# A transformer block, forward and backward: dq kept in SBUF for half of the tokens, the dqkv transposes moved ahead of the last stage, dx interleaved with the last dWqkv pass

## The chip, the cores and the metric

The kernel runs on one core of a Trainium2 chip. The metric is device time in microseconds, the median of several runs. A core has TensorE (PE: matmuls, and PEld: weight loads), VectorE (DVE), ScalarE (ACT), GpSimd (POOL) and SyncE (SP); matmuls write to PSUM, all else lives in SBUF or in DRAM. In this kernel three engines issue DMAs: SP (`LD`), ACT (`AQ`) and POOL (`ST`).

## The reference

One pre-LN block with its gradients, in bf16: sequence S = 2048, width D = 512, 32 heads of 16, MLP width F = 1792. Attention of a token looks at W = 8 tokens, two apart: `idx = pos[:, None] - 2 * arange(8)[None, :]`, masked below zero.

```python
h = x + _A_ref(_layernorm(x), A_wqkv, A_wo)
h2 = h + _B_ref(_layernorm(h), B_w1, B_b1, B_w2, B_b2)   # gelu MLP
```

The kernel returns h2 and the gradients dx, dWqkv, dWo, dW1, db1, dW2, db2. At the end of the backward pass, with ln1 the normalized x: dq = sum over the window of ds times k; dWqkv = ln1^T [dq dk dv]; dln1 = [dq dk dv] Wqkv^T; and dx is the LayerNorm backward of dln1, plus dh.

## The kernel before, in words

A token tile is 128 tokens on 128 partitions, so there are NT = 16 of them, and NPR = 8 pairs. D makes DT = 4 tiles of 128, 3D makes JT = 12. The program runs through stages: LN1 and a weight permutation, QKV and attention with LN2 (phases B and C), the MLP forward and backward (D), dW2, dWo and dO, then four stages that matter here.

**H (L706 to L795)** goes through the pairs and forms ds, which stays in SBUF (`ds_tiles`), and dk and dv, by matmuls with shift matrices into PSUM (`sacc`), an ACT cast (`res_sb`, L722) and a POOL store to DRAM (`dk_d`, `dv_d`).

**dW1** is spread over H and E2 by two helpers. `d3b_load` (L592) loads a 128x512 piece of dh1 on ACT's queue (`dh1c`, L600) and transposes it on TensorE (`tpd`). `d3b_mm` (L604) does one of 16 output blocks: 16 matmuls (L617), an ACT cast (`dw_sb`, L620) and a POOL store (L621). Their buffers are in the pools of the stack `d3`, on the right side of SBUF, closed at L833.

**E2 (L802 to L832)** forms dq. For each pair it loads KL (L812, eight loads of 256 KB on SP, one for each window position, two buffers); for each of the two tiles VectorE multiplies by ds (`pk`, L817), adds eight terms to four (L821), to two (L823), to one (`dq_sb`, L825), and POOL stores the tile to `dq_d` (L826). Two blocks of dW1 follow each pair. After pair 2, 16 loads on ACT's queue (L831) bring ln1 back as `xh1_tm`.

**K (L839 to L910)** comes when E2's and d3's pools are closed. It loads the weights `wqp` (L848) and dk (L851) on SP, dv on ACT (L853), and dq half on POOL, half on SP (L855), as column blocks of `dqkv_tm[st]`, one [128, 1536] tile for each token tile. Twelve groups of four TensorE transposes make WqkvT. Then the loop over `jc in [1, 2, 0]` (dk, dv, dq): for each token tile, four matmuls into the four banks of one PSUM tile `dwqkv_ps` (L865) and one group of four transposes of the same block into `dqkvT`, and after 16 tiles four casts, on ACT (L872) and VectorE (L874) by turns, and four POOL stores (L875). At last 16 dx tiles: twelve matmuls into `dln_ps` (L880), an ACT pass that sums rows (L891), six VectorE instructions (L894 to L908) and a POOL store (L910).

A group of transposes goes through `pe_T` (L130): four transposes into one PSUM tile (`tps`, two buffers), then one copy to SBUF by ACT or VectorE (L135).

The order on each engine is the scheduler's, which places instructions by their dependences and priorities; it is not always the program's order. In the profile and the order, `xh` is xh1_tm, `ln_d` is ln1_d and ln2_d, `dqkv` a tile of dqkv_tm, `t` the partial sums of E2.

Of the kernel before, what the change touches and what calls it, by code (L numbers as in the profile page):

```python
# [38 lines left out]
def build(ctx, tc, A_x, A_wqkv, A_wo, B_w1, B_b1, B_w2, B_b2, grad_out,  # L39
# [762 lines left out]
    with tc.tile_pool(name="i_big", bufs=2) as i_big, \  # L802
            tc.tile_pool(name="i_pv", bufs=2) as i_pv, \
            tc.tile_pool(name="i_t", bufs=2) as i_t, \
            tc.tile_pool(name="i_io", bufs=4) as i_io, \
            tc.tile_pool(name="ps_w1b", bufs=2, space=bass.MemoryType.PSUM) as ps_w1b:
        for pr in range(NPR):
            tok0 = pr * PS2
            KL = i_big.tile([P, W, 2, D], BF16, name="KL")
            for w in range(W):  # L810
                r0 = PAD + tok0 - 2 * w
                LD.dma_start(out=KL[:, w, :, :], in_=k_tm_d[r0:r0 + PS2, :].rearrange("(k p) d -> p k d", p=P))  # L812
            for k in range(2):
                t = pr * 2 + k
                ts0 = t * P
                pk = i_pv.tile([P, W, DH, H], BF16, name="pk")
                nc.vector.tensor_tensor(out=pk[:], in0=KL[:, :, k, :].rearrange("p w (d h) -> p w d h", d=DH, h=H),  # L817
                                        in1=ds_tiles[t][:, :, None, :].to_broadcast([P, W, DH, H]), op=ALU.mult)
                pk3 = pk[:].rearrange("p w d h -> p w (d h)")
                t1 = i_t.tile([P, 4, D], BF16, name="t1")  # L820
                nc.vector.tensor_tensor(out=t1[:], in0=pk3[:, 0:4, :], in1=pk3[:, 4:8, :], op=ALU.add)  # L821
                t2 = i_t.tile([P, 2, D], BF16, name="t2")
                nc.vector.tensor_tensor(out=t2[:], in0=t1[:, 0:2, :], in1=t1[:, 2:4, :], op=ALU.add)  # L823
# [3 lines left out]
                dbg_tm('dq', t, r_sb[:], i_io)  # L827
            d3b_mm(2, ps_w1b)
            if pr == 2:
                for st in range(NT):  # L830
                    AQ.dma_start(out=xh1_tm[st][:], in_=ln1_d[st * P:(st + 1) * P, :])  # L831
        d3b_mm(len(d3_work), ps_w1b)  # L832
    d3.close()  # L833
    if dbg.get('stop_after') == 'E':
        fpre_cm.__exit__(None, None, None)
        dsp_cm.__exit__(None, None, None)
        return

    with tc.tile_pool(name="k_w", bufs=1) as k_w, \  # L839
# [9 lines left out]
        dqkv_tm = [k_w.tile([P, 3 * D], BF16, name=f"dqkv_{i}") for i in range(NT)]  # L849
        for st in range(NT):  # L850
            LD.dma_start(out=dqkv_tm[st][:, D:2 * D], in_=dk_d[st * P:(st + 1) * P, :])  # L851
        for st in range(NT):
            AQ.dma_start(out=dqkv_tm[st][:, 2 * D:3 * D], in_=dv_d[st * P:(st + 1) * P, :])  # L853
        for st in range(NT):
            (nc.gpsimd if st % 2 == 0 else LD).dma_start(out=dqkv_tm[st][:, 0:D], in_=dq_d[st * P:(st + 1) * P, :])  # L855
# [4 lines left out]
        dqkvT = k_w.tile([P, JT, S], BF16, name="dqkvT")  # L860
        for jc in [1, 2, 0]:
            dw_ps = ps_kw.tile([P, DT, D], F32, name="dwqkv_ps")
            for st in range(NT):
                for ct in range(DT):
                    nc.tensor.matmul(dw_ps[:, ct, :], lhsT=xh1_tm[st][:, ct * P:(ct + 1) * P],  # L865
                                     rhs=dqkv_tm[st][:, jc * D:(jc + 1) * D], start=(st == 0), stop=(st == NT - 1))
# [2 lines left out]
            for ct in range(DT):
                w_sb = k_io.tile([P, D], BF16, name="dwqkv_sb")  # L870
                if ct % 2 == 0:
                    nc.scalar.copy(out=perm_view(w_sb[:]), in_=dh_view(dw_ps[:, ct, :]))  # L872
                else:
                    nc.vector.tensor_copy(out=perm_view(w_sb[:]), in_=dh_view(dw_ps[:, ct, :]))  # L874
                ST.dma_start(out=out_dwqkv[ct * P:(ct + 1) * P, jc * D:(jc + 1) * D], in_=w_sb[:])  # L875
        for t in range(NT):
# [92 lines left out]
```

## Time and profile before

| | us |
|---|---|
| median of 5 runs | 1091.3 |
| lowest and highest | 1087.05, 1096.33 |
| profiled execution | 1092.42 |
| its span, first to last instruction | 1090.7 |
| granted TensorE clock, mean over the span | 0.890 |

The profile is one execution; times in it count from the start of its span. A row of the timeline has start, length, engine, line, operation, tile written and tiles read, a count, and in brackets the idle time ahead of it and what ended that. ACTq and SPq are the DMA issues of those queues.

### The profile page before, as it was taken

How to read it: one execution, taken by the hardware profiler on the slowest of the kernel's cores; microseconds unless marked ns; L12 is line 12 of the kernel's file. 1: busy time of each engine (PE TensorE's matmuls, PEld its weight loads, DVE VectorE, ACT ScalarE, POOL GpSimd, SP SyncE). 2: the span in 40 equal slices, each digit the busy share in tenths (PEclk: the TensorE clock that was granted, in tenths of full speed). 3: DMA queues.
4: the chain of work that ended last, by engine and by line, in shares of the span. 5: the costliest groups of instructions: out<-in, count | busy, mean ns of one | idle time of the engine just before them, and what ended most of it. 6: DMA issues, size and time to landing. Idle time of an engine off the chain costs nothing. (4 is left out here: it accounts for less than half of the span.)

```text
span 1090.7 us, 14749 instructions
## 1 busy us (share of the span) xinstructions
PE 813.4 (75%) x5145; PEld 401.5 (37%) x5234; DVE 703.1 (64%) x1448; ACT 415.6 (38%) x745; POOL 214.5 (20%) x402
## 2 busy tenths in 40 slices
...
GB/s 256 145 174 155 244 156 196 183 130 83 11 44 98 54 87 68 36 96 40 49 111 63 109 172 46 94 80 81 97 66 59 314 311 246 224 90 20 20 77 68
DMA packets 102893, 126.87 MB, mean 116 GB/s; under 512 B 14977, under 2 KB 90530, under 8 KB 102818
## 3 DMA queue, kind: packets, MB, share of 16 engines
...
q14 instruction: 34, 0.28, 0.1%
...
## 5 line engine op out<-in xcount | busy, mean ns | idle before, releaser
L421 PE MATMUL dl_ps<-w1T,dh 128*128 128x512 bf16 x217 | 63.1, 413 | 17.9 <-DVE t L443 17.3
...
L479 PE MATMUL h_ps<-ln2T_all,w 128*128 128x512 bf16 x220 | 62.1, 387 | 6.4 <-ACT c1u L484 4.7
L518 PE MATMUL dg_ps<-dYTg,w2T 128*128 128x512 bf16 x216 | 62.2, 381 | 5.7 <-DVE db1part L521 4.8
L500 PE MATMUL y_ps<-w,gch 128*128 128x512 bf16 x218 | 58.0, 384 | 5.3 <-DVE gch L496 4.8
L701 PE MATMUL sacc<-pvE,SC 128*128 128x512 bf16 x223 | 57.0, 398 | 0.2 <-issue 0.2
L695 PE MATMUL sacc<-pvE,SD 128*128 128x512 bf16 x203 | 52.3, 393 | 6.3 <-DVE pvE L786 5.4
L135 ACT COPY dh_tmA<-tpd 128x512 bf16<-128x512 bf16 x56 | 32.5, 586 | 64.2 <-PE tpd L134 61.8
L880 PE MATMUL dln_ps<-wqkvT,dqkvT 128*128 128x512 bf16 x187 | 47.3, 400 | 10.9 <-DVE k_t L903 10.3
L617 PE MATMUL dw_ps<-dh_tmA,ln_tm 128*128 128x512 bf16 (+1 forms) x241 | 52.6, 361 | 2.7 <-ACT dw_sb L620 0.8
L134 PE MATMUL tps<-ident,xhat 128*128 128x128 bf16 x128 | 16.3, 275 | 49.1 <-DVE xhat L177 34.2
L865 PE MATMUL dwqkv_ps<-dqkv,xh 128*128 128x512 bf16 x184 | 52.0, 409 | 1.0 <-DMA dqkv<-dk_d 0.5
L323 PE MATMUL acc<-pv,ident 128*128 128x512 bf16 x123 | 40.0, 474 | 15.0 <-DVE pv L319 14.6
L817 DVE TENSOR_TENSOR pk<-KL,ds_t 128x4096 bf16<-128x4096 bf16 x16 | 35.9, 2285 | 23.1 <-DMA KL<-k_tm_d 21.8
L722 ACT CAST res_sb<-sacc 128x512 bf16<-128x512 f32 x32 | 18.7, 585 | 82.7 <-PE sacc L695 76.2
L482 ACT ACTIVATE u<-h_ps,b1col 128x512 bf16<-128x512 f32 x56 | 38.3, 685 | 19.1 <-DMA w<-in_B_w_dram 5.9
L277 DVE TENSOR_TENSOR prod<-kTg,qTg 128x1024 bf16<-128x1024 bf16 x64 | 40.0, 678 | 7.1 <-ACT kTg L236 7.1
L134 PE MATMUL tpd<-ident,dh1c 128*128 128x128 bf16 x224 | 24.1, 234 | 27.3 <-DMA dh1c<-dh_d 18.6
L521 DVE CUSTOM_DVE_ANT_0 dh<-dg_ps,gd 128x512 bf16<-128x512 f32 x56 | 38.3, 684 | 7.3 <-PE dg_ps L518 6.6
L747 DVE TENSOR_TENSOR prodA<-vT,doT 128x1024 bf16<-128x1024 bf16 x64 | 42.3, 681 | 0.5
L421 PEld LDWEIGHTS <-dh 128*128 128x128 bf16 x224 | 23.2, 104 | 47.4 <-issue 26.6
L319 DVE TENSOR_TENSOR pv<-VL,a_bf 128x4096 bf16<-128x4096 bf16 x16 | 36.3, 2278 | 6.5 <-DMA VL<-v_tm_d 3.7
...
## 6 DMA issues: line engine op xcount, KB each, us to landing
VL<-v_tm_d SPq DMA_DIRECT2D x64, 256.0 KB, 5.2
KL<-k_tm_d SPq DMA_DIRECT2D x64, 256.0 KB, 5.4
dh_d<-dh POOLq DMA_DIRECT2D x72, 128.0 KB, 2.1
dh1c<-dh_d ACTq DMA_DIRECT2D x56, 128.0 KB, 2.4
x_sb<-in_A_x_dram SPq DMA_DIRECT2D x32, 128.0 KB, 3.6
ln_d<-xhat POOLq DMA_DIRECT2D x32, 128.0 KB, 2.8
dh_r<-dh_d SPq DMA_DIRECT2D x32, 128.0 KB, 2.2
out_dram<-dw_sb POOLq DMA_DIRECT2D x26, 128.0 KB, 2.4
```

The costliest lines, as they stand in the source:

```text
L134: nc.tensor.transpose(ps[:, i, :], s, ident[:])
L277: nc.vector.tensor_tensor(out=prt[:], in0=win, in1=qT[:, jt:jt + 1, s_off:s_off + PS2].to_broadcast([P, 4, PS2]), op=ALU.mult)
L421: nc.tensor.matmul(dl_ps[:], lhsT=dh1_list[ft][:, tt * P:(tt + 1) * P], rhs=W1T_sb[ft][:], start=(ft == 0), stop=(ft == FT - 1))
L479: nc.tensor.matmul(h1_ps[:], lhsT=W1_sb[ct][:, ft * P:(ft + 1) * P], rhs=ln2T_all[:, ct, sc * GS:(sc + 1) * GS], start=(ct == 0), stop=(ct ...
L500: nc.tensor.matmul(y_ps[:, tt, :], lhsT=gch[:, tt * P:(tt + 1) * P], rhs=W2_sb[ft][:], start=(ft == 0), stop=False)
L518: nc.tensor.matmul(dg_ps[:], lhsT=W2T_sb[dt][:, ft * P:(ft + 1) * P], rhs=dYTg[:, dt, :], start=(dt == 0), stop=(dt == DT - 1))
L617: nc.tensor.matmul(ps[:, 0:fl], lhsT=ln2_tm[st][:, ct * P:(ct + 1) * P], rhs=dh1_tmA[:, st, f0:f0 + fl], start=(st == 0), stop=(st == NT - 1))
L695: nc.tensor.matmul(acc_list[t - 1][:], lhsT=SDm[w][:], rhs=rhs[w], start=False, stop=(w == W - 1))
L701: nc.tensor.matmul(acc_list[t][:], lhsT=SC[w][:], rhs=rhs[w], start=(w == 0), stop=(last_tile and w == W - 1))
L747: nc.vector.tensor_tensor(out=prt[:], in0=win, in1=doT[:, jt:jt + 1, tok0:tok0 + PS2].to_broadcast([P, 4, PS2]), op=ALU.mult)
L865: nc.tensor.matmul(dw_ps[:, ct, :], lhsT=xh1_tm[st][:, ct * P:(ct + 1) * P], rhs=dqkv_tm[st][:, jc * D:(jc + 1) * D], start=(st == 0), sto ...
L880: nc.tensor.matmul(dl_ps[:], lhsT=dqkvT[:, jt, ts0:ts0 + P], rhs=WqkvT[:, jt, :], start=(jt == 0), stop=(jt == JT - 1))
```

## The change

1. E2's body becomes a function, `e2_pair(pr, keep_pool)`. Pairs 0 to 3 store dq to DRAM as before, with three dW1 blocks after each pair. Pairs 4 to 7 write dq straight into the first 512 columns of `dqkv_tm[t]`. The partial sums have one buffer in place of two, `dq_sb` three in place of four.
2. The xh1 loads go from ACT's queue to SP's, after pair 1 in the program.
3. When d3 is closed, a new pool `ftr` on the right side holds `dqkvT` and `dqkv_tm`; the loads of dk (16), dv (16) and dq of the first eight tiles are all issued on ACT there.
4. The 48 groups of dqkv transposes go out of K's loop to between pairs 4 to 7; the twelve of WqkvT stay in K.
5. `dwqkv_ps` becomes four tiles of one bank each.
6. A dx tile becomes a function, called eleven times within the dq pass of dWqkv (from st = 5 on), five times after it.

The core of the diff (the indented bodies that only moved are left out):

```diff
-    with tc.tile_pool(name="i_big", bufs=2) as i_big, \
...
-            tc.tile_pool(name="i_t", bufs=2) as i_t, \
-            tc.tile_pool(name="i_io", bufs=4) as i_io, \
...
+    i_t = e2.enter_context(tc.tile_pool(name="i_t", bufs=1))
+    i_io = e2.enter_context(tc.tile_pool(name="i_io", bufs=3))
...
+    def e2_pair(pr, keep_pool):
...
+            if keep_pool is not None:
+                nc.vector.tensor_tensor(out=keep_pool[t][:, 0:D], in0=t2[:, 0, :], in1=t2[:, 1, :], op=ALU.add)
+            else:
                 r_sb = i_io.tile([P, D], BF16, name="dq_sb")
                 nc.vector.tensor_tensor(out=r_sb[:], in0=t2[:, 0, :], in1=t2[:, 1, :], op=ALU.add)
                 ST.dma_start(out=dq_d[ts0:ts0 + P, :], in_=r_sb[:])
...
-            d3b_mm(2, ps_w1b)
-            if pr == 2:
+        for pr in range(4):
+            e2_pair(pr, None)
+            d3b_mm(3, ps_w1b)
+            if pr == 1:
                 for st in range(NT):
-                    AQ.dma_start(out=xh1_tm[st][:], in_=ln1_d[st * P:(st + 1) * P, :])
+                    LD.dma_start(out=xh1_tm[st][:], in_=ln1_d[st * P:(st + 1) * P, :])
         d3b_mm(len(d3_work), ps_w1b)
     d3.close()
+    ftr_cm = tc.tile_pool(name="ftr", bufs=1, side="right")
+    ftr = ftr_cm.__enter__()
+    dqkvT = ftr.tile([P, JT, S], BF16, name="dqkvT")
+    dqkv_tm = [ftr.tile([P, 3 * D], BF16, name=f"dqkv_{i}") for i in range(NT)]
+    for st in range(NT):
+        AQ.dma_start(out=dqkv_tm[st][:, D:2 * D], in_=dk_d[st * P:(st + 1) * P, :])
+    for st in range(NT):
+        AQ.dma_start(out=dqkv_tm[st][:, 2 * D:3 * D], in_=dv_d[st * P:(st + 1) * P, :])
+    for st in range(8):
+        AQ.dma_start(out=dqkv_tm[st][:, 0:D], in_=dq_d[st * P:(st + 1) * P, :])
...
+        for pr in range(4, NPR):
+            e2_pair(pr, dqkv_tm)
+            for st in range((pr - 4) * 4, (pr - 4) * 4 + 4):
+                tr_st(st, [1, 2])
+            for st in range((pr - 4) * 2, (pr - 4) * 2 + 2):
+                tr_st(st, [0])
+        for st in range(8, NT):
+            tr_st(st, [0])
...
-        for jc in [1, 2, 0]:
-            dw_ps = ps_kw.tile([P, DT, D], F32, name="dwqkv_ps")
...
-                pe_T(ps_kt, [dqkv_tm[st][:, jc * D + i * P:jc * D + (i + 1) * P] for i in range(DT)],
-                     dqkvT[:, jc * DT:(jc + 1) * DT, st * P:(st + 1) * P], SCc if (st + jc) % 2 == 0 else VC)
...
+        for jc in [1, 2, 0]:
+            dw_l = [ps_kw.tile([P, D], F32, name=f"dwqkv_ps{ct}") for ct in range(DT)]
+            for st in range(NT):
...
+                if jc == 0 and st >= 5:
+                    dx_tile(n_dx)
+                    n_dx += 1
...
+        for t in range(n_dx, NT):
+            dx_tile(t)
```

What the scheduler makes of it is seen at three places. The first is VectorE in the second half of E2 (`ds_t_6984` is the ds of tile 10, the first of pair 5; `dqkv_10123` is dqkv_tm[8]). Before:

```order
L817 TENSOR_TENSOR pk<-KL,ds_t_6984 128x4096
L817 TENSOR_TENSOR pk<-KL,ds_t_6985 128x4096
L821 TENSOR_TENSOR t_10105<-pk 128x2048
L821 TENSOR_TENSOR t_10114<-pk 128x2048
L823 TENSOR_TENSOR t_10107<-t_10105 128x1024
L823 TENSOR_TENSOR t_10116<-t_10114 128x1024
L825 TENSOR_TENSOR dq_sb<-t_10107 128x512
L825 TENSOR_TENSOR dq_sb<-t_10116 128x512
L817 TENSOR_TENSOR pk<-KL,ds_t_6986 128x4096
```

After, at the same place:

```order
L819 TENSOR_TENSOR pk<-KL,ds_t_6984 128x4096
L823 TENSOR_TENSOR t_10192<-pk 128x2048
L819 TENSOR_TENSOR pk<-KL,ds_t_6985 128x4096
L827 TENSOR_TENSOR dqkv_10123<-t_10187 128x512
L825 TENSOR_TENSOR t_10194<-t_10192 128x1024
L827 TENSOR_TENSOR dqkv_10124<-t_10194 128x512
L823 TENSOR_TENSOR t_10268<-pk 128x2048
L135 COPY dqkvT<-tps 128x4x128
L825 TENSOR_TENSOR t_10270<-t_10268 128x1024
L819 TENSOR_TENSOR pk<-KL,ds_t_6986 128x4096
```

The last step of pair 4 has come behind the products of pair 5, writes into dqkv_tm, whose memory was d3's, and a copy of transposes stands among the work of pair 5.

The second place is ACT at the end of the loads (`dqkv_10263` and `dqkv_10264` are the last two tiles of dqkv_tm before, `dqkv_10121` and `dqkv_10122` tiles 6 and 7 after). Before:

```order
L853 DMA dqkv_10263<-dv_d 128x512
L853 DMA dqkv_10264<-dv_d 128x512
L135 COPY wqkvT<-tps 128x512 x6
L135 COPY dqkvT<-tps 128x4x128 x7
L872 CAST dwqkv_sb<-dwqkv_ps 128x16x32
```

After:

```order
L851 DMA dqkv_10121<-dq_d 128x512
L851 DMA dqkv_10122<-dq_d 128x512
L135 COPY dqkvT<-tps 128x4x128 x5
L934 CAST dwqkv_sb<-dwqkv_ps_10658 128x16x32
L135 COPY dqkvT<-tps 128x4x128
```

Ahead of these rows ACT now has 40 load issues in a row, from the last dW1 casts on; before it had the 16 of dv. The copies behind the loads are now those of dqkv transposes, with the first dWqkv casts among them; before, they were those of the weights' transposes. On SP nine xh1 loads now go ahead of the first 16 loads of KL, seven behind them, and then come the other 48 and wqp.

The third place is TensorE at the last token tile of the dq pass (`xh_15_9599` is xh1_tm[15]). Before:

```order
L865 LDWEIGHTS xh_15_9599
L865 MATMUL dwqkv_ps<-dqkv_10264,xh_15_9599 128x512
L134 LDWEIGHTS dqkv_10264
L134 MATMUL tps<-ident,dqkv_10264 128x128
...
L880 LDWEIGHTS dqkvT
L880 MATMUL dln_ps<-wqkvT,dqkvT 128x512
```

After:

```order
L890 MATMUL dln_ps<-wqkvT,dqkvT 128x512
L926 LDWEIGHTS xh_15_9599
L926 MATMUL dwqkv_ps_10818<-dqkv_10130,xh_15_9599 128x512
L926 LDWEIGHTS xh_15_9599
L926 MATMUL dwqkv_ps_10819<-dqkv_10130,xh_15_9599 128x512
L926 LDWEIGHTS xh_15_9599
L926 MATMUL dwqkv_ps_10820<-dqkv_10130,xh_15_9599 128x512
L926 LDWEIGHTS xh_15_9599
L926 MATMUL dwqkv_ps_10821<-dqkv_10130,xh_15_9599 128x512
L890 LDWEIGHTS dqkvT
L890 MATMUL dln_ps<-wqkvT,dqkvT 128x512
```

The four matmuls of a tile have a bank each, there are no transposes among them, and dx's matmuls stand on both sides: ten dx tiles lie between the dWqkv steps of tiles 5 and 15, and six come after them. On TensorE before the first wqp transposes there are now the whole jc = 1 pass and eight groups of dqkv transposes; the other 40 groups and the twelve of wqp stand among the first half of the jc = 2 pass.

More of the change, by code (lines that the diff above doesn't have):

```diff
@@ L801, in build @@
     xh1_tm = [fpre.tile([P, D], BF16, name=f"xh1_{i}") for i in range(NT)]
-    with tc.tile_pool(name="i_big", bufs=2) as i_big, \
-            tc.tile_pool(name="i_pv", bufs=2) as i_pv, \
-            tc.tile_pool(name="i_t", bufs=2) as i_t, \
-            tc.tile_pool(name="i_io", bufs=4) as i_io, \
[L806 to L823, printed above, removed]
@@ L844, in build @@
             tc.tile_pool(name="ps_kw", bufs=1, space=bass.MemoryType.PSUM) as ps_kw, \
-            tc.tile_pool(name="ps_kt", bufs=2, space=bass.MemoryType.PSUM) as ps_kt:
+            tc.tile_pool(name="ps_kt3", bufs=2, space=bass.MemoryType.PSUM) as ps_kt3:
         wqp = k_w.tile([P, DT, 3 * D], BF16, name="wqp")
@@ L848, in build, with dx_tile @@
             LD.dma_start(out=wqp[:, ct, :], in_=wqkvp_d[ct * P:(ct + 1) * P, :])
[L849 to L855, printed above, removed]
         WqkvT = k_w.tile([P, JT, D], BF16, name="wqkvT")
         for jt in range(JT):
-            pe_T(ps_kt, [wqp[:, ct, jt * P:(jt + 1) * P] for ct in range(DT)],
+            pe_T(ps_kt3, [wqp[:, ct, jt * P:(jt + 1) * P] for ct in range(DT)],
                  WqkvT[:, jt, :].rearrange("p (a b) -> p a b", a=DT), SCc if jt % 2 == 0 else VC)
-        dqkvT = k_w.tile([P, JT, S], BF16, name="dqkvT")
-        for jc in [1, 2, 0]:
-            dw_ps = ps_kw.tile([P, DT, D], F32, name="dwqkv_ps")
[L863 to L866, printed above, removed]
-                pe_T(ps_kt, [dqkv_tm[st][:, jc * D + i * P:jc * D + (i + 1) * P] for i in range(DT)],
-                     dqkvT[:, jc * DT:(jc + 1) * DT, st * P:(st + 1) * P], SCc if (st + jc) % 2 == 0 else VC)
[L869 to L876, printed above, removed]
+        def dx_tile(t):
             ts0 = t * P
```

41 lines of the change are left out of this document (40 added, 1 removed).

## The prediction

> **What bounds the kernel now.** The page comes first, for the span and the engines.
>
> ```profile
> span 1090.7 us, 14749 instructions
> PE 813.4 (75%) x5145; PEld 401.5 (37%) x5234; DVE 703.1 (64%) x1448; ACT 415.6 (38%) x745; POOL 214.5 (20%) x402
> ```
>
> TensorE leads, but 75% is a mean over stages. The change touches only what follows 840 us, so the second view is a table of windows there (columns: window, length, busy us of PE, PEld, DVE, ACT, POOL with counts, granted TensorE clock, DMA share, GB/s).
>
> ```profile
> 850.00:900.00 50.00, 29.82 (x158) 14.60 (x159) 39.48 (x35) 11.06 (x20) 8.57 (x16) 0.82 0.96 313
> 912.00:938.00 26.00, 0.00 (x0) 0.00 (x0) 19.11 (x21) 0.65 (x2) 7.08 (x14) 0.58 0.48 159
> 938.00:950.00 12.00, 2.01 (x10) 0.82 (x11) 0.42 (x1) 0.00 (x0) 2.51 (x5) 0.50 1.05 361
> 1000.00:1009.00 9.00, 5.42 (x27) 3.17 (x28) 5.55 (x5) 5.26 (x6) 2.16 (x4) 0.59 0.14 46
> 1036.00:1086.00 50.00, 40.55 (x164) 16.83 (x167) 46.74 (x111) 9.63 (x28) 8.64 (x16) 0.91 0.24 77
> ```
>
> To 900 us VectorE (dq) and the DMA engines are the busy ones. From 912 to 950 TensorE has 2 us of work: first VectorE finishes dq alone, then the DMA engines fetch at 361 GB/s. Around 1004 TensorE waits for casts out of PSUM. After 1036 VectorE bounds, busy 46.74 of 50 us. The timeline and the chain of waits name what ended each stretch.
>
> ```profile
> 906.70 4.75 PE L617 MATMUL dw_ps<-dh_tmA,ln_tm 128*128 128x256 bf16 x40 [0.24 <-ACT dh_tmA L135]
> 914.37 0.54 POOL L621 DMA_DIRECT2D out_dram<-dw_sb  x1
> 933.09 2.03 DMA dq_d<-dq_sb
> 935.64 15.20 ACTq L853 DMA_DIRECT2D dqkv<-dv_d  x16
> 938.98 0.37 PE L134 MATMUL tps<-ident,wqp 128*128 128x128 bf16 x2 [27.53 <-DMA dqkv<-dv_d]
> 944.59 11.04 SPq L851 DMA_DIRECT2D dqkv<-dk_d  x16
> 949.54 0.58 PE L865 MATMUL dwqkv_ps<-dqkv,xh 128*128 128x512 bf16 x1 [0.53 <-DMA dqkv<-dk_d]
> 998.76 2.30 ACT L872 CAST dwqkv_sb<-dwqkv_ps 128x512 bf16<-128x512 f32 x1 [0.28 <-PE dwqkv_ps L865]
> 1005.78 2.32 DVE L874 CAST dwqkv_sb<-dwqkv_ps 128x512 bf16<-128x512 f32 x1 [1.03 <-ACT dwqkv_sb L872]
> 1008.31 4.06 PE L865 MATMUL dwqkv_ps<-dqkv,xh 128*128 128x512 bf16 x10
> 1080.49 0.81 DVE L903 TENSOR_SCALAR k_t<-dln_ps,rstd,k_nm 128x512 f32<-128x512 f32 x1
> 1083.46 0.81 DVE L903 TENSOR_SCALAR k_t<-dln_ps,rstd,k_nm 128x512 f32<-128x512 f32 x1
> 1085.02 0.75 DVE L908 SCALAR_TENSOR_TENSOR dx<-xh,k_nm,k_t 128x512 bf16<-128x512 bf16 x1
> ```
>
> TensorE ends dW1 at 911.45 (906.70 plus 4.75). The last dq store lands at 935.12; only then are dv and dk issued, and the first dWqkv matmul comes at 949.54. The four casts of one dw_ps tile follow one another from 998.76 to 1008.10, and matmuls resume at 1008.31, at half speed. Dx tiles come 2.97 us apart (1080.49, 1083.46), and VectorE ends at 1085.77, 4.9 before the span's end.
>
> **The change, part by part.** Times are on the span's clock of before. The profiled execution took 1092.42 us, so 1.7 lie around its span; the median of the runs, 1091.3, is 1.1 lower.
>
> *Step 1: start of E2, and the end E of dW1.* These rows price it; the last is of the waits (total, times, longest).
>
> ```profile
> 840.79 1.29 ACTq L831 DMA_DIRECT2D xh<-ln_d  x3
> 852.82 1.07 ACT L620 CAST dw_sb<-dw_ps 128x512 bf16<-128x512 f32 x2 [7.25 <-DMA xh<-ln_d]
> 859.27 4.49 DVE L817 TENSOR_TENSOR pk<-KL,ds_t 128x4096 bf16<-128x4096 bf16 x2 [18.51 <-DMA KL<-k_tm_d]
> 867.83 4.49 DVE L817 TENSOR_TENSOR pk<-KL,ds_t 128x4096 bf16<-128x4096 bf16 x2
> PE tpd L134 <- DMA dh1c<-dh_d: 18.6, 6, 8.6
> ```
>
> The 16 xh1 loads leave ACT, whose dW1 cast waited 7.25 us behind their issues. On SP nine of them go ahead of the first KL loads, in time that the queue spends waiting for KL's buffers, and seven behind two pairs of KL. The first pk comes some 4 us sooner, at 855. A pair takes 8.56 us (859.27 to 867.83), so pairs 0 to 4 and the two pk of pair 5 run to 855 + 42.8 + 5 = 903. TensorE waited 18.6 us in dW1 for dh1c, once 8.6, while xh1 crowded the same DMA engines. At best that long wait goes (E = 903), at worst nothing (911.5); I take half, E = 907.5, since KL comes sooner and crowds too.
>
> The Trainium skill ("DMA: Bandwidth & Descriptors", Issuing engines are not separate DMA queues) says that another issuing engine saves only the issue time. By that rule E would be near 911, and the sum 3 us higher; no row here shows xh1 on SP.
>
> *Step 2: the gate G, a wait that is new.* dqkv_tm and dqkvT now lie where d3's buffers were, so the first dk load and VectorE's first write into dqkv wait until the last dW1 store has landed.
>
> ```profile
> 912.11 0.65 ACT L620 CAST dw_sb<-dw_ps 128x256 bf16<-128x256 f32 x2 [3.92 <-DMA out_dram<-dw_sb]
> out_dram<-dw_sb POOLq DMA_DIRECT2D x4, 64.0 KB, 3.8
> ```
>
> Cast 0.65, store 0.54 and landing up to 3.8 (the second row's median) give G = E + 4.5 = 912. The casts' wait of 3.92 for a store buffer shrinks with eight dq stores gone from the queue. VectorE is at the gate from 903, so 9 us of E2 are held there, and behind that write on its queue all that is left of E2; on ACT, behind the first of 40 loads, stand the other 39 and then the copies of the transposes.
>
> *Step 3: loads, the rest of E2, and jc=1.* The DMA view (kind, count, size, median us to landing) has the loads, the timeline three rows of a step of before.
>
> ```profile
> KL<-k_tm_d SPq DMA_DIRECT2D x64, 256.0 KB, 5.4
> dqkv<-dk_d SPq DMA_DIRECT2D x16, 128.0 KB, 3.3
> wqp<-wqkvp_d SPq DMA_DIRECT2D x4, 384.0 KB, 4.5
> dqkv<-dq_d SPq DMA_DIRECT2D x8, 128.0 KB, 3.5
> 961.04 0.39 PE L134 MATMUL tps<-ident,dqkv 128*128 128x128 bf16 x4
> 961.26 1.03 PE L865 MATMUL dwqkv_ps<-dqkv,xh 128*128 128x512 bf16 x4
> 962.12 0.39 PE L134 MATMUL tps<-ident,dqkv 128*128 128x128 bf16 x4
> ```
>
> Four transposes hold TensorE for 0.22 us (961.04 to 961.26), a matmul for 0.215 (0.86 / 4), at half clock 0.44 and 0.43. Xh1's three issues took 0.43 us each (1.29 / 3), dk's 16 alone 0.69 (11.04), dv's 0.95 (15.20) beside two other queues. I take 0.5, the middle of the first two: 40 loads end at G + 20. By bytes: 40 loads of 128 KB, eight KL of 256 KB for pair 7 make 7.3 MB, 20 us at 361 GB/s, which agrees. Of E2's 68.5 us (eight pairs) VectorE has 20.6 left; 2.2 of them run before a first copy that needs dk0 (G + 4.4, 3.3 of it landing), the other 18.4 end at G + 23. Wqp waits for the last pk, some 2 us sooner, and lands near G + 26 = 938. TensorE's 64 jc=1 matmuls need 13.8, at half clock 27.5; the last can't start before dk's sixteenth load, so they are done between G + 22 and G + 32, and the transposes in line behind them start between G + 22 and there; I take wqp's 938 for the start of step 4. Before, jc=1 began at 949.54; this step is the larger gain. Sixteen dq trips to DRAM become eight, off the path.
>
> *Step 4: the transposes, and jc=2.* They were hidden: a step of four dW matmuls and four transposes, 1.08 us (961.04 to 962.12), kept TensorE full. Now they run by themselves, and the copies out of two PSUM buffers set their pace.
>
> ```profile
> 955.27 0.58 ACT L135 COPY wqkvT<-tps 128x512 bf16<-128x512 bf16 x1 [0.47 <-PE tps L134]
> 956.33 0.59 ACT L135 COPY wqkvT<-tps 128x512 bf16<-128x512 bf16 x1 [0.47 <-PE tps L134]
> ```
>
> Two groups of four, one on ACT and one on VectorE, take 1.06 us. After 938 some 52 groups are left (twelve of wqp, 40 of dqkv): 27.5 us, to 965, with the first 32 jc=2 matmuls in their gaps and jc=1's casts too. The other 32 take 6.9: 972. Before, jc=2 was done at 998.7. Here the change gives back what hid the transposes (27.5 against 52 x 0.22 = 11.4 on TensorE), and pays it from jc=1's early start.
>
> *Step 5: jc=2's casts, jc=0 and dx.* With one bank per tile, two casts on ACT and two on VectorE run side by side: 4.6 us, not 9.3. TensorE needs 9.6 from 972 to the end of jc=0's step 5 (24 matmuls 5.2, and 4.4 of waiting for the fourth cast, which needs a store's buffer): 981.6. Then ten dx tiles of 12 matmuls (one matmul is already issued) take turns with the ten dW steps of 4 that are left: 159 x 0.215 = 34.2, to 1016. A round takes 3.4 us, and VectorE needs 2.97 for a dx tile, so it keeps up. Two jc=0 casts on VectorE (4.6), six tiles (17.8) and a first tile's way through (some 3.6) end at 1042, against 1085.77.
>
> *Step 6: clock and tail.* The wait of 4.4 us before jc=0 will be followed by half clock, as 1000 to 1009 was (0.59): about 9 us at half speed cost 4.5. The tail stays 4.9. The sum: 1042 + 4.5 + 4.9 = 1051.4 of span, 1053.1 with 1.7 around it, and 1052 against the median.
>
> **Rivals.** *Cold transposes.* Step 4 leaves TensorE with 0.22 of work per 0.53 us, and step 3 begins after an idle of several us, so the clock may stay half through step 4. At half speed 52 groups and 32 matmuls fill 52 x 0.44 + 32 x 0.43 = 36.6 us rather than 27.5, and the next 32 cost 7 more: +16, 1068. Against it stands the nearest window, with a group within it (953 to 958):
>
> ```profile
> 952.00:958.00 6.00, 5.73 (x47) 3.45 (x47) 1.88 (x5) 2.34 (x4) 0.00 (x0) 0.85 0.94 277
> L134 PE MATMUL tps<-ident,wqp 128*128 128x128 bf16 x36 | 3.7, 229 | 0.1
> ```
>
> With 36 transposes among some 47 matmuls the clock rose there from 0.50 to full; but dW matmuls stood between them. The Trainium skill ("TensorE: Matmul & The Clock Gate", Part 4: PE-mode transpose) holds that transposes don't count as a busy TensorE, which speaks for this rival; that row doesn't bear it out. Chance 0.12.
>
> *Crowded loads.* The 40 loads go at dv's pace, 0.95 us: ACT is free for its first copy at G + 38, and the last dq lands some 3.5 later, at 953 rather than 938: +15, 1067. For it: pair 7's KL and wqp compete. Against: two queues, not three. Chance 0.08; with cold transposes too (1083) 0.02.
>
> *No gate cost.* E = 903, and no cold stretch before jc=0: 1052 - 4.5 - 4.5 = 1043. Chance 0.08.
>
> *Slower: the loads in front of the copies.* ACT must issue all 40 before it copies one transpose, and dx needs the last. At x us a load, the copies begin at G + 40x + 3.5 in place of G + 26. The whole gain, 39 us, is gone at x = (39 + 22.5) / 40 = 1.54, and from 1.68 on the kernel is slower by over 0.5%: 1097 and up. Dearest row: 0.95. Chance 0.03. Between 1.40 and 1.68 it is no change, and so it is if the interleaved stretch of step 5 is cold for its whole length (159 matmuls at 0.43, 34 us more): 0.03 together.
>
> **How the numbers follow.** The forecast has 0.64. The low end is the no-gate case with 5 us more for loads at 0.43 and shorter waits: 1038. The high end takes in both single rivals and half of their sum: 1076. Left out: 0.03, 0.03, 0.02 and some 0.08 of the rest. About 0.5%, 5.5 us, is what a measurement of this kernel can tell from no change. Faster: 0.64 + 0.12 + 0.08 + 0.02 + 0.08 = 0.94; same 0.03; slower 0.03.
>
> **What would show it.** Right: TensorE's last L617 near 907; VectorE stopped at a write into dqkv from 903 to 912; the ACT queue's loads done near 932; jc=1's matmuls ahead of 940; copies of transposes every 0.53 us to about 965; casts in pairs; dx tiles from 985 on; a last dx near 1046. Wrong: loads at 0.9 us each; clock at 0.5 between 938 and 972 or between 990 and 1016; rounds of step 5 well over 3.4 us, which would say that VectorE or PSUM bounds them and that six tiles are not all that is left behind.

## The result, and the profile after

The changed kernel takes 1049.69 us (median of 9 runs, 1043.95 to 1051.71), the kernel before 1090.89 (15 runs). The ratio is 0.9623, with a 95% interval of 0.9603 to 0.9644: 41 us less. The forecast was 1052, in a range of 1038 to 1076. The profiled execution took 1051.26 us. Its page begins:

```profile
span 1049.5 us, 14709 instructions
PE 814.8 (78%) x5146; PEld 402.2 (38%) x5234; DVE 706.0 (67%) x1448; ACT 415.9 (40%) x745; POOL 205.9 (20%) x386
```

Busy times hardly moved: TensorE 814.8 after 813.4, VectorE 706.0 after 703.1. What went is idle time. The windows of the end (columns as before: busy of PE, PEld, DVE, ACT, POOL, then granted TensorE clock, DMA share, GB/s) show where:

```profile
912.00:938.00 26.00, 18.52 (x72) 8.19 (x75) 20.49 (x21) 0.65 (x2) 0.00 (x0) 0.74 0.85 260
938.00:968.00 30.00, 24.28 (x259) 17.35 (x263) 18.75 (x36) 20.32 (x31) 2.15 (x4) 0.94 0.27 88
975.00:984.00 9.00, 5.69 (x25) 2.40 (x25) 4.37 (x2) 4.02 (x2) 2.15 (x4) 1.00 0.17 58
984.00:1018.00 34.00, 33.84 (x157) 15.35 (x158) 27.81 (x63) 6.43 (x19) 4.32 (x8) 1.00 0.20 63
1018.00:1046.00 28.00, 18.24 (x74) 7.55 (x73) 25.43 (x52) 8.89 (x16) 6.17 (x12) 0.93 0.23 76
```

From 912 to 938 TensorE now has 18.5 us of work beside VectorE's 20.5, where it had none. The stretch from 938 to 968 is new: almost only transposes on TensorE, at clock 0.94. From 984 to 1018 TensorE is full. The timeline has the turning points:

```profile
903.11 4.75 PE L617 MATMUL dw_ps<-dh_tmA,ln_tm 128*128 128x256 bf16 x40 [0.19 <-ACT dh_tmA L135]
909.76 0.65 ACT L620 CAST dw_sb<-dw_ps 128x256 bf16<-128x256 f32 x2 [5.17 <-DMA out_dram<-dw_sb]
912.90 11.03 ACTq L847 DMA_DIRECT2D dqkv<-dk_d  x16
913.14 0.42 DVE L827 TENSOR_TENSOR dqkv<-t 128x512 bf16<-128x512 bf16 x1 [5.32 <-DMA out_dram<-dw_sb]
916.01 7.70 PE L926 MATMUL dwqkv_ps<-dqkv,xh 128*128 128x512 bf16 x27 [0.22 <-issue]
924.04 8.33 ACTq L849 DMA_DIRECT2D dqkv<-dv_d  x16
932.41 4.89 ACTq L851 DMA_DIRECT2D dqkv<-dq_d  x8
937.35 1.07 ACT L135 COPY dqkvT<-tps 128x512 bf16<-128x512 bf16 x2 [26.94 <-DMA dqkv<-dq_d]
938.57 0.61 PE L134 MATMUL tps<-ident,dqkv 128*128 128x128 bf16 x8
967.64 7.50 PE L926 MATMUL dwqkv_ps<-dqkv,xh 128*128 128x512 bf16 x34
974.98 0.38 PE L890 MATMUL dln_ps<-wqkvT,dqkvT 128*128 128x512 bf16 x1
976.93 0.59 PE L926 MATMUL dwqkv_ps<-dqkv,xh 128*128 128x512 bf16 x2 [1.57 <-ACT dwqkv_sb L934]
979.07 5.20 PE L926 MATMUL dwqkv_ps<-dqkv,xh 128*128 128x512 bf16 x21 [1.55 <-ACT dwqkv_sb L934]
984.11 2.54 PE L890 MATMUL dln_ps<-wqkvT,dqkvT 128*128 128x512 bf16 x11
1018.43 2.75 PE L890 MATMUL dln_ps<-wqkvT,dqkvT 128*128 128x512 bf16 x12
1044.70 0.75 DVE L918 SCALAR_TENSOR_TENSOR dx<-xh,k_nm,k_t 128x512 bf16<-128x512 bf16 x1
```

Against the rows of before, the 41.2 us of span divide so:

| piece | before | after | change |
|---|---|---|---|
| first dWqkv matmul starts | 949.5 | 916.0 | -33.5 |
| from there to the end of the dv pass | 49.0 (to 998.5) | 59.0 (to 975.0) | +10.0 |
| to the first matmul of the dq pass | 9.8 (to 1008.3) | 1.9 (to 976.9) | -7.9 |
| to VectorE's last dx | 77.5 (to 1085.8) | 68.5 (to 1045.4) | -9.0 |
| to the end of the span | 4.9 | 4.1 | -0.8 |

The early start brought most. Ten of its 33.5 us went back in the next piece: it holds 29 us in which the transposes stand almost alone, while the turn between the dk and dv passes, where the kernel before cast for 9.3 us (972.1 to 981.4), is gone.

### The profile page after: what moved, and what is told of

Its sections match the earlier page's. It is cut to its first block, busy times and chain, and to the rows that moved or that the text cites. A ratio compares the mean times of both kernels' runs of the same rounds, so it can differ in the third digit from the quotient of the medians.

```text
span 1049.5 us, 14709 instructions
## 1 busy us (share of the span) xinstructions
PE 814.8 (78%) x5146; PEld 402.2 (38%) x5234; DVE 706.0 (67%) x1448; ACT 415.9 (40%) x745; POOL 205.9 (20%) x386
## 5 line engine op out<-in xcount | busy, mean ns | idle before, releaser
L421 PE MATMUL dl_ps<-w1T,dh 128*128 128x512 bf16 x217 | 62.5, 410 | 18.5 <-DVE t L443 17.9
L617 PE MATMUL dw_ps<-dh_tmA,ln_tm 128*128 128x512 bf16 (+1 forms) x241 | 54.1, 371 | 1.9 <-ACT res_sb L722 0.7
L926 PE MATMUL dwqkv_ps<-dqkv,xh 128*128 128x512 bf16 x183 | 49.5, 408 | 6.1 <-ACT dwqkv_sb L934 5.4
L819 DVE TENSOR_TENSOR pk<-KL,ds_t 128x4096 bf16<-128x4096 bf16 x16 | 36.5, 2286 | 21.7 <-DMA KL<-k_tm_d 19.9
L890 PE MATMUL dln_ps<-wqkvT,dqkvT 128*128 128x512 bf16 x189 | 45.2, 388 | 4.6 <-DVE k_t L913 4.3
L492 ACT ACTIVATE sg<-inner 128x512 bf16<-128x512 bf16 x56 | 35.3, 630 | 12.1 <-DVE inner L490 10.7
```

The source lines that it names most:

```text
L421: nc.tensor.matmul(dl_ps[:], lhsT=dh1_list[ft][:, tt * P:(tt + 1) * P], rhs=W1T_sb[ft][:], start=(ft == 0), stop=(ft == FT - 1))
L617: nc.tensor.matmul(ps[:, 0:fl], lhsT=ln2_tm[st][:, ct * P:(ct + 1) * P], rhs=dh1_tmA[:, st, f0:f0 + fl], start=(st == 0), stop=(st == NT - 1))
L890: nc.tensor.matmul(dl_ps[:], lhsT=dqkvT[:, jt, ts0:ts0 + P], rhs=WqkvT[:, jt, :], start=(jt == 0), stop=(jt == JT - 1))
L926: nc.tensor.matmul(dw_l[ct][:], lhsT=xh1_tm[st][:, ct * P:(ct + 1) * P], rhs=dqkv_tm[st][:, jc * D:(jc + 1) * D], start=(st == 0), stop=(s ...
```

## The experiments

In the kernels that issue xh1 on SP, dW1's last matmul (E) ended anywhere from 900.3 to 907.9 in one profiled execution each (ten of them), although next to nothing had been changed ahead of it. A single span therefore says little about what comes later. Beside the time, the table gives the length from ACT's issue of the first dk load (the gate, G) to the span's end, called the stretch: 136.6 in the changed kernel (912.90 to 1049.5). It too comes from one execution each, and it moves by about a microsecond where nothing behind the gate was changed (e1). An early gate does not lengthen it by itself: in the six kernels whose loads and transposes are those of the changed one (it, e1, e2, e3, n2, n3), the last group of transposes starts 53.5 to 54.3 us after G, for G from 904.8 to 918.1. Ratios are to the kernel before.

| run | median us | ratio, interval | E | G | G to end |
|---|---|---|---|---|---|
| changed kernel | 1049.69 | 0.9623, 0.9603 to 0.9644 | 907.9 | 912.9 | 136.6 |
| e1_xh1_act | 1052.36 | 0.9651, 0.9624 to 0.9677 | 913.1 | 918.1 | 135.3 |
| e2_one_tile | 1057.29 | 0.9692, 0.9663 to 0.9720 | 907.6 | 912.9 | 142.5 |
| e3_dx_after | 1052.03 | 0.9643, 0.9617 to 0.9670 | 904.0 | 908.8 | 141.0 |
| e4_dq_dram | 1056.88 | 0.9693, 0.9665 to 0.9721 | 907.9 | 913.0 | 143.2 |
| e5_dq_dram_pool | 1053.36 | 0.9656, 0.9623 to 0.9689 | 901.3 | 906.1 | 141.5 |
| n1_pool_loads | 1053.31 | 0.9651, 0.9610 to 0.9692 | 900.3 | 905.1 | 141.5 |
| n2_casts_act | 1051.83 | 0.9646, 0.9617 to 0.9675 | 907.0 | 912.5 | 139.6 |
| n3_casts_gate | 1049.87 | 0.9617, 0.9586 to 0.9648 | 900.5 | 904.8 | 137.8 |
| n4_double_copies | 1048.70 | 0.9609, 0.9581 to 0.9637 | 903.0 | 907.9 | 138.2 |
| n5_cast_order | 1036.37 | 0.9495, 0.9460 to 0.9530 | 907.3 | 911.7 | 126.6 |
| e6_before_banks | 1078.27 | 0.9892, 0.9858 to 0.9926 | | | |
| e7_before_banks_dx | 1075.60 | 0.9864, 0.9832 to 0.9896 | | | |

**e1_xh1_act**: xh1 back on ACT's queue.

```diff
-            if pr == 1:
+            if pr == 2:
                 for st in range(NT):
-                    LD.dma_start(out=xh1_tm[st][:], in_=ln1_d[st * P:(st + 1) * P, :])
+                    AQ.dma_start(out=xh1_tm[st][:], in_=ln1_d[st * P:(st + 1) * P, :])
```

> The changed kernel with part 2 undone: the 16 xh1 loads are issued on ACT's queue after pair 2, as before. Theory (the loads crowd dh1c and hold ACT's casts, step 1): dW1's last matmul goes from 907.9 back to about 911, the gate with it, and the time rises by 3 us, to about 1053. Rival (only the issue time counts, what the Trainium skill, DMA: Bandwidth & Descriptors, Issuing engines are not separate DMA queues, says): the last dW1 matmul moves by under 1 us and the time stays within 1 us of 1049.7.

The timeline and the waits of e1:

```profile
845.79 8.62 ACTq L839 DMA_DIRECT2D xh<-ln_d  x8
854.50 1.07 ACT L620 CAST dw_sb<-dw_ps 128x512 bf16<-128x512 f32 x2 [8.15 <-DMA xh<-ln_d]
PE tpd L134 <- DMA dh1c<-dh_d: 17.0, 4, 9.6
DVE pk L819 <- DMA KL<-k_tm_d: 23.9, 3, 20.6
```

ACT's casts are held again and the first KL comes later (20.6 of waiting; the changed kernel's longest wait for KL is 15.4). E is 913.1, outside the ten of 900.3 to 907.9, and the ratio is 0.0028 higher, 3 us. The size is the theory's, but the two intervals overlap: likely, not settled.

**e2_one_tile**: one PSUM tile of four banks.

```diff
-            dw_l = [ps_kw.tile([P, D], F32, name=f"dwqkv_ps{ct}") for ct in range(DT)]
+            dw_ps = ps_kw.tile([P, DT, D], F32, name="dwqkv_ps")
```

> The changed kernel with part 5 undone: the four banks of dWqkv are one PSUM tile again. Theory (separate tiles let ACT and VectorE cast side by side, and matmuls into a bank start when that bank is free): the four casts follow one another again, 9.3 us; TensorE waits some 9 us instead of 3.1 ahead of the dq pass, or fills the wait with dx matmuls, and VectorE's casts at the end come later: 5 to 12 us more, 1055 to 1062. Rival (the interleaved dx and transposes fill that wait, so the banks bring nothing): within 2 us of 1049.7.

The casts ahead of the dq pass, in e2's timeline:

```profile
976.61 2.32 ACT L934 CAST dwqkv_sb<-dwqkv_ps 128x512 bf16<-128x512 f32 x1 [8.49 <-PE dwqkv_ps L926]
978.96 2.30 DVE L936 CAST dwqkv_sb<-dwqkv_ps 128x512 bf16<-128x512 f32 x1 [10.78 <-ACT dwqkv_sb L934]
981.29 2.29 ACT L934 CAST dwqkv_sb<-dwqkv_ps 128x512 bf16<-128x512 f32 x1 [2.37 <-DVE dwqkv_sb L936]
983.62 2.29 DVE L936 CAST dwqkv_sb<-dwqkv_ps 128x512 bf16<-128x512 f32 x1 [2.36 <-ACT dwqkv_sb L934]
985.97 7.64 PE L926 MATMUL dwqkv_ps<-dqkv,xh 128*128 128x512 bf16 x28 [5.73 <-DVE dwqkv_sb L936]
986.00:991.00 5.00, 5.00 (x17) 1.95 (x18) 2.86 (x7) 0.00 (x0) 1.08 (x2) 0.71 0.23 79
```

One cast waits for the other again, as before the change. TensorE fills part of the wait with 17 dx matmuls, then stands 5.73 us, and the clock is 0.71 in the 5 us behind it. The cost is 7.5 us of time (0.9692 against 0.9623, intervals apart) and 5.9 in the stretch, within the theory's 5 to 12.

**e3_dx_after**: `if jc == 0 and st >= 5:` becomes `if False:`, so all 16 dx tiles come last.

> The changed kernel with part 6 undone: all 16 dx tiles come after the dq pass. Theory (dx is bound by VectorE at 2.97 us a tile, so interleaving gains only VectorE's idle time in ten dW steps, less the slower rounds): the dq pass ends near 993, 16 tiles take 47.5, casts and the first tile's way some 8: VectorE ends near 1049 to 1052 and not at 1045.5, the time is 3 to 7 us more, 1053 to 1057. Rival (interleaving hides the matmuls of ten dx tiles, 26 us): 1065 or more.

Its stretch is 4.4 us longer, within the theory's 3 to 7, but the time only 2 us (0.9643, the intervals overlap), below its 1053 to 1057. Part of the 4.4 need not come from dx's place: in the 6 us from 974.87 the clock was 0.72, where the changed kernel had 1.00 at the same point, and that is 1.7 us. So 2 to 3 us are left for interleaving. TensorE in e3's timeline:

```profile
974.87 15.23 PE L926 MATMUL dwqkv_ps<-dqkv,xh 128*128 128x512 bf16 x62 [1.55 <-ACT dwqkv_sb L934]
1008.68 2.75 PE L890 MATMUL dln_ps<-wqkvT,dqkvT 128*128 128x512 bf16 x12 [0.22 <-DVE k_t L913]
1011.65 2.75 PE L890 MATMUL dln_ps<-wqkvT,dqkvT 128*128 128x512 bf16 x12 [0.22 <-DVE k_t L913]
```

Tiles come 2.97 us apart, each waiting for VectorE, as before. Interleaving gains little because VectorE needs some 47.5 us for 16 tiles (16 x 2.97) wherever they stand.

**e4_dq_dram and e5_dq_dram_pool**: dq of pairs 4 to 7 goes through DRAM again, in e4 with its loads on SP (the diff), in e5 on POOL (`ST` for `LD`).

```diff
-            e2_pair(pr, dqkv_tm)
+            e2_pair(pr, None)
...
         for st in range(8, NT):
+            LD.dma_start(out=dqkv_tm[st][:, 0:D], in_=dq_d[st * P:(st + 1) * P, :])
+        for st in range(8, NT):
             tr_st(st, [0])
```

> The changed kernel with part 1's core undone: dq of pairs 4 to 7 is stored to DRAM as before and loaded again on SP's queue; early loads and transposes stay. Theory (dq's trip is off the path, since its transposes are done only by 967 and dq itself by 945): within 2 us of 1049.7. It also takes VectorE's write away from the gate, so E2 need not stop at 908; by the theory that is worth little, because TensorE is paced by the loads then. Rival (the DRAM trip of the last dq was the wait that held everything, 933 to 950 before): 5 us more or worse.

In e4's timeline SP stood at a dq load ahead of the last KL loads, and wqp came late:

```profile
913.77 0.33 SPq L864 DMA_DIRECT2D dqkv<-dq_d  x1
940.37 1.27 SPq L883 DMA_DIRECT2D wqp<-wqkvp_d  x3
```

The queue that I chose could be the cost, so e5 takes the loads off SP.

> As e4_dq_dram, but the eight dq loads of pairs 4 to 7 go out on POOL's queue, behind their own stores, so that SP's loads of KL and wqp are not held. In e4 SP's first dq load stood at 913.8 ahead of the last eight KL loads, and wqp came 5 us late. Theory (dq's DRAM trip is off the path, and e4's 7 us came from the queue that I put the loads on): within 2 us of 1049.7. Rival (the trip itself costs: more DMA in the crowded stretch, and the last dq late): again 5 us or more above it.

The stretch is still 4.9 us longer than the changed kernel's, and the time 3.6 us (0.9656 against 0.9623, intervals overlapping), between the theory's 2 and the rival's 5. ACT's loads in e5:

```profile
906.10 12.89 ACTq L847 DMA_DIRECT2D dqkv<-dk_d  x16
933.35 1.07 ACT L135 COPY dqkvT<-tps 128x512 bf16<-128x512 bf16 x2 [30.43 <-DMA dqkv<-dq_d]
```

ACT is free 27.2 us after the first dk load, not 24.5, and the last transposes come 58.0 us after it, not 54.1. My theory, that dq's trip is off the path, falls by the stretch. The trip's latency is hidden, but its transfers go among the loads that ACT must issue before it can copy: in the first 24.4 us after G the DMA engines moved 7.20 MB in e5, with eight of the trip's 16 transfers and one more load of KL, and 6.54 MB in the changed kernel; ACT had issued 36 of its 40 loads there, not all 40. In e4 the last transposes come as late as in e5 (58.1), so the queue cost nothing up to there; e4's stretch is longer by another 1.7 us, as much as its clock of 0.72 in the 6 us from 983.20 costs (e5 has 1.00 at that point). By the medians e4 is 3.5 us behind e5, with overlapping intervals, so a cost of the queue is not excluded.

**e6_before_banks and e7_before_banks_dx** put parts 5, and 5 and 6, into the kernel before; the last three lines of the diff are e7's alone.

```diff
-            dw_ps = ps_kw.tile([P, DT, D], F32, name="dwqkv_ps")
+            dw_l = [ps_kw.tile([P, D], F32, name=f"dwqkv_ps{ct}") for ct in range(DT)]
...
+                if jc == 0 and st >= 5:
+                    dx_tile(n_dx)
+                    n_dx += 1
```

> The kernel before with part 5 alone: four PSUM tiles of one bank in place of one of four. Theory (each of the three turns between the passes waited some 9.5 us for four casts in a row): each turn shrinks by 4 to 6 us, and the half clock behind it with it: 1091 less 14 to 20, that is 1071 to 1077. Rival (the banks only pay together with the rest): within 3 us of 1091.

> The kernel before with parts 5 and 6 alone: one-bank tiles, and eleven dx tiles called within the dq pass; loads, dq through DRAM and transposes stay as before. Theory (interleaving dx is worth the 4.5 us that e3 showed from the end of the dv pass on, and starting loads early and overlapping E2 the rest): 3 to 6 us below e6_before_banks, so that parts 1 to 4 bring the remaining 17 to 25 of the 40 us. Rival (dx interleaved brings more here, since TensorE carries transposes in that pass too): 10 us or more below e6.

Banks alone bring 12 us (0.9892), a little less than the 14 to 20 expected; the timeline of e6 between the first two passes shows one reason:

```profile
970.60 4.44 ACT L872 CAST dwqkv_sb<-dwqkv_ps 128x512 bf16<-128x512 f32 x2 [0.72 <-PE dwqkv_ps L865]
970.82 2.30 DVE L874 CAST dwqkv_sb<-dwqkv_ps 128x512 bf16<-128x512 f32 x1
976.60 0.43 DVE L135 COPY dqkvT<-tps 128x512 bf16<-128x512 bf16 x1 [3.48 <-PE tps L134]
976.95 2.29 DVE L874 CAST dwqkv_sb<-dwqkv_ps 128x512 bf16<-128x512 f32 x1
```

Casts start side by side, but VectorE's second starts 3.8 us after its first has ended, behind a copy of transposes that waits 3.48 us for TensorE. Interleaving adds 3 (0.9864), with overlapping intervals. So, added in this order, parts 1 to 4 bring the other 26 of 41 us (0.9864 to 0.9623), a little more than the 17 to 25 expected. No run takes the early loads and transposes (parts 3 and 4) apart.

**n1_pool_loads**: dv and dq loads on POOL.

```diff
-        AQ.dma_start(out=dqkv_tm[st][:, 2 * D:3 * D], in_=dv_d[st * P:(st + 1) * P, :])
+        ST.dma_start(out=dqkv_tm[st][:, 2 * D:3 * D], in_=dv_d[st * P:(st + 1) * P, :])
     for st in range(8):
-        AQ.dma_start(out=dqkv_tm[st][:, 0:D], in_=dq_d[st * P:(st + 1) * P, :])
+        ST.dma_start(out=dqkv_tm[st][:, 0:D], in_=dq_d[st * P:(st + 1) * P, :])
```

> The changed kernel with the 16 dv and 8 dq loads issued on POOL's queue, idle then, and only dk's 16 on ACT. ACT's queue is free at 924 and not at 937, so it copies transposes of dk and dv while E2 ends; the scheduler puts some 17 copies each of ACT and VectorE there. Theory (step 4: the transposes stand alone from 938.6 to 967.6 because ACT could not copy earlier): that stretch shrinks by 8 to 14 us while VectorE's part of the copies delays E2 by some 8 that nothing waits for: 1036 to 1042. Rival (DMA bandwidth, not ACT's issue, sets when the transposes can go; copies on VectorE delay the last dq): within 3 us of 1049.7, or slower.

```profile
905.11 16.14 ACTq L847 DMA_DIRECT2D dqkv<-dk_d  x16
905.76 5.83 POOL L849 DMA_DIRECT2D dqkv<-dv_d  x11 [2.69 <-DMA KL<-k_tm_d]
922.55 0.42 DVE L135 COPY dqkvT<-tps 128x512 bf16<-128x512 bf16 x1 [9.12 <-PE tps L134]
```

With POOL loading beside it, ACT's 16 loads took 16.1 us and not 11.0; VectorE, with a copy next on its queue, stood 9.1 us for a transpose that waited for ACT's first copy; and the last pk came 35 us after the first dk load, not 19, and wqp with it. The stretch is 4.9 longer, the time 3.0 (intervals overlapping). The rival was right in the outcome, and for its second reason: copies placed in E2 delay E2, which wqp waits for. Its first is half true. With two queues all 40 loads were issued within 19.8 us, not 24.4, and ACT was free 16.2 us after the first; the DMA share in those 19.8 us was 0.99, against 0.88 in the 24.4 us of the changed kernel. So ACT's one queue was part of what set the pace in the changed kernel, and in n1 little bandwidth was left to gain.

**n2_casts_act**: `if ct % 2 == 0:` becomes `if ct % 2 == 0 or jc == 0:`.

> The changed kernel with the four casts of the dq pass all on ACT, none on VectorE. Theory (step 5: VectorE bounds the end, and its two casts of 2.3 us each stand between dx tiles while ACT waits for 37 us): VectorE ends 3 to 4.6 us sooner, 1045 to 1047. Rival (ACT's four casts in a row, 9.2 us, hold back its dl_bf pass, so that VectorE waits for that instead): within 1.5 us of 1049.7.

```profile
1018.15 8.81 ACT L934 CAST dwqkv_sb<-dwqkv_ps 128x512 bf16<-128x512 f32 x4
1027.51 0.69 DVE L904 CUSTOM_DVE_ANT_0 k_prodx<-dl_bf,xh 128x512 bf16<-128x512 bf16 x1 [6.03 <-ACT dl_bf L901]
```

The rival's mechanism again: ACT's four casts in a row kept VectorE waiting 6.03 us for the next dl_bf. The stretch is 3.0 us longer; the time is 2.5 us longer (0.9646, overlapping), a little above the rival's 1.5.

**n3_casts_gate** adds `bufs=4` to dW1's store pool `f3_io`.

> As n2_casts_act, and four store buffers in place of two for dW1's output. Theory (step 2: the last dW1 casts waited 5.17 us for a store to land, so the gate opened 5.0 us after the last matmul and not 3): the last casts follow the last matmul at once, the gate opens some 2 us sooner, and the time falls by as much again: 1043 to 1045. Rival (what follows the gate is paced by bandwidth or by wqp, which waits for E2): no more than n2_casts_act.

The time shows no gain over n2 that a measurement could tell (0.9617 against 0.9646, overlapping), and the stretch starts behind the gate. The last casts did follow the last matmul: they ended 0.45 us after it instead of 2.55. But from E to G it took 4.3 us (4.9 and 4.4 in n4 and n5, which have the four buffers too), against 4.8 to 5.5 in the kernels with two: the landing of the last store holds the gate more than the buffer does.

**n4_double_copies**: transposes in eights.

```diff
+        def tr_2(st):
+            pe_T(ps_kt, [dqkv_tm[st][:, D + i * P:D + (i + 1) * P] for i in range(2 * DT)],
+                 dqkvT[:, DT:3 * DT, st * P:(st + 1) * P], SCc if st < 6 or st % 2 == 0 else VC)
...
-                tr_st(st, [1, 2])
+                tr_2(st)
```

> As n3_casts_gate, and the transposes of dk and dv of a token tile, and of two tiles of WqkvT, go through one PSUM tile of eight and are copied in one instruction: 38 copies in place of 60. The first two dv loads go out behind the first two of dk, and the first six double copies are ACT's, so that VectorE doesn't wait for them in E2. Theory (step 4: the stretch from 938.6 to 967.6 is set by the turn of transposes, semaphore and copy in two buffers, not by the engines' throughput, since ACT is busy 0.58 and VectorE 0.42 of 1.06 us): 20 double copies at some 0.8 us apart in place of 40 at 0.53 save 4 to 6 us: 1038 to 1041. Rival (a copy of 1024 takes twice as long as one of 512 and the stretch is bound by the copies): within 1.5 us of n3_casts_gate.

A double copy on each engine, in n4's timeline:

```profile
948.78 1.01 ACT L135 COPY dqkvT<-tps 128x1024 bf16<-128x1024 bf16 x1 [0.69 <-PE tps L134]
949.22 0.69 DVE L135 COPY dqkvT<-tps 128x1024 bf16<-128x1024 bf16 x1 [0.42 <-PE tps L134]
```

The last transposes come 51.0 us after the first dk load, not 53.6 as in n3 or 54.1 as in the changed kernel: 3 us gained, less than expected, since ACT's copy of 1024 took 1.01 us, against 0.59 of one of 512. Behind them the gain was lost: ACT's four casts at the end cost 3.0 us in n2, and the clock in the 6 us behind the casts ahead of the dq pass was 0.72 (1.00 in the changed kernel), which costs 1.7 (columns as in the windows above):

```profile
972.28:978.28 6.00, 6.00 (x20) 2.37 (x20) 2.31 (x1) 0.00 (x0) 1.08 (x2) 0.72 0.15 53
```

The time is the changed kernel's, and within the rival's 1.5 us of n3.

**n5_cast_order**: n4 with n2's edit undone, and the casts walking in the order of the output (ACT's in the diff, VectorE's likewise).

```diff
-                    nc.scalar.copy(out=perm_view(w_sb[:]), in_=dh_view(dw_l[ct][:]))
+                    nc.scalar.copy(out=w_sb[:].rearrange("p (h d) -> p h d", h=H, d=DH),
+                                   in_=dw_l[ct][:].rearrange("p (d h) -> p h d", d=DH, h=H))
```

> As n4_double_copies, but with the casts of the dq pass again by turns on ACT and VectorE, and all twelve dWqkv casts walking in the order of the output: they write contiguously and read PSUM in steps, where they read contiguously and wrote in steps of 16 elements. Theory (the 2.3 us of such a cast, against 0.585 for ACT's plain cast of 128x512, come from the stepped write): a cast takes 0.6 to 0.8 us; TensorE's wait ahead of the dq pass (3.1 us) nearly goes, VectorE gets back 3.3 us at the end, and the double copies keep their 3 us: the stretch from the first dk load to the span's end falls from 136.6 us to 127 to 130, and the time to 1040 to 1043. Rival (a step on either side costs the same): casts stay at 2.3 us, the stretch at 134 to 136, the time at 1046 to 1049.

The casts in groups (count, busy, mean ns), first of the changed kernel:

```profile
L936 DVE CAST dwqkv_sb<-dwqkv_ps 128x512 bf16<-128x512 f32 x6 | 14.0, 2329 | 9.4 <-PE dwqkv_ps L926 6.7 <-DMA out_dram<-dwqkv_sb 2.7
L934 ACT CAST dwqkv_sb<-dwqkv_ps 128x512 bf16<-128x512 f32 x6 | 13.7, 2455 | 6.6 <-PE dwqkv_ps L926 6.6
```

then of n5:

```profile
L943 DVE CAST dwqkv_sb<-dwqkv_ps 128x512 bf16<-128x512 f32 x6 | 4.1, 690 | 11.9 <-PE dwqkv_ps L932 8.0 <-DMA out_dram<-dwqkv_sb 3.8
L940 ACT CAST dwqkv_sb<-dwqkv_ps 128x512 bf16<-128x512 f32 x6 | 3.3, 591 | 7.8 <-PE dwqkv_ps L932 7.8
972.04 0.38 PE L896 MATMUL dln_ps<-wqkvT,dqkvT 128*128 128x512 bf16 x1
972.25 5.68 PE L932 MATMUL dwqkv_ps<-dqkv,xh 128*128 128x512 bf16 x23
```

The same 512 elements take 0.59 us on ACT and 0.69 on VectorE instead of 2.3 to 2.5, TensorE goes from the dv pass to the dq pass without a wait, and the stretch is 126.6. This version beats both kernels: 1036.37 us, ratio 0.9495 (0.9460 to 0.9530), 1.3% under the changed kernel (0.9495 / 0.9623). The time was better than the theory's 1040 to 1043. Against n4 it gains 12 us, but that step also undoes n2's edit. Against the changed kernel it gains 14.0 us of time and 10.0 of stretch, with the 3 us of the double copies in it, so I estimate the casts' order alone at 7 to 11 us.

## Why the prediction was right, point by point

Times on the span's clock, forecast first.

- *Step 1, E:* 907.5, and 907.9 in this execution. That it is so near is luck in part: E lay between 900.3 and 907.9 in ten executions, 904.7 in their mean. e1 bears out the reason (xh1 off ACT's queue) in size. The Trainium skill's rule that another issuing engine saves only the issue time ("DMA: Bandwidth & Descriptors", Issuing engines are not separate DMA queues) had E near 911, as the prediction read it; e1's 913.1 and 3 us speak against that reading, without settling it. The issue time itself was not small here: eight xh1 issues held ACT for 8.62 us, and a dW1 cast behind them waited 8.15. VectorE reached the gate at 907.8, not 903: it had waited for KL three times, 19.9 us in all, 15.4 of them ahead of the first pk.
- *Step 2, the gate:* 912, and 912.9. The wait was there and named as foreseen (5.32 us on VectorE, for dW1's store). The 5.17 us that the last casts waited for a store buffer did not shrink, and did not matter (n3).
- *Step 3, loads:* 40 loads in 20 us, and it took 24.4 (912.90 to 937.3): 0.69, 0.52 and 0.61 us each for dk, dv and dq. This term was mis-sized by 4 us. Part of that was a slip: the middle of 0.43 and 0.69 is 0.56, not 0.5, and gives 22.4. e5 shows that more transfers in this stretch slow the loads, and n1 that a second queue speeds them; how much of the 24.4 is bandwidth and how much ACT's one queue stays open. Transposes began at 938.57, forecast 938, and that was luck: I had taken wqp's landing for the start, but the first transpose of wqp came only at 941.37, and what the transposes waited for was ACT, free at 937.35 and not at 932.
- *Step 4:* 27.5 us for the transposes, and 29.1 (938.57 to 967.64); then 32 matmuls to 975.0, forecast 972.
- *Step 5:* 9.6 us to step 5's end, and 9.1 (to 984.11); 34.2 for the rounds, and 34.3; 26 for the end, and 27.0 (1018.43 to 1045.45). The theory behind it, that VectorE bounds dx and interleaving is worth a few us only, held in e3 and e7.
- *Step 6, the clock:* 4.5 us, and none in this execution: 1.00 from 975 to 1018, with waits of 1.57 and 1.55 us and matmuls between. This is the term that failed outright, in two ways. Its size was too large. In e2, with one wait of 5.73, the clock fell to 0.71 over 5 us: 1.5 us, a third of what I took. And of the half clock before the change, most of 1000 to 1009 lay within the wait itself; behind it only 3.7 us were slow (the window below), about 1.8 us of cost. That it was nothing at all is luck in part: nine kernels have the same two waits (1.49 to 1.57 us each), and in the 6 us behind the second the clock was 1.00 in six of them, but 0.72 in e3, e4 and n4. The tail was 4.1, not 4.9.

The window behind that wait, in the kernel before:

```profile
1008.30:1012.00 3.70, 3.70 (x13) 1.34 (x11) 0.05 (x1) 0.58 (x1) 0.54 (x1) 0.52 0.10 35
```

So the sum was near because errors cancelled: +3.4 up to VectorE's end (1045.4 against 1042), -4.5 for the clock, -0.8 for the tail. The cause was as forecast. What I called off the path was not quite: *"Sixteen dq trips to DRAM become eight, off the path"* costs 3.6 us of time and 4.9 of the stretch when undone (e5). Of the rivals, cold transposes fell: a window of the changed kernel with 104 matmuls, 100 of them transposes, has clock 0.93.

```profile
949.00:958.00 9.00, 7.82 (x104) 6.81 (x105) 6.70 (x13) 6.51 (x12) 0.54 (x1) 0.93 0.12 40
```

The rule in the Trainium skill that spoke for that rival ("TensorE: Matmul & The Clock Gate", Part 4: PE-mode transpose) does not hold in this window. Crowded loads did not come: the dearest were 0.69 us each (dk). In n1 ACT's 16 took 1.0 us each, but beside POOL's 24, and ACT was free the sooner for it.

What stays open: why E varies by 7 us between executions, why the clock fell behind the same waits in three executions and not in six, and the exact worth of xh1's queue.
